# Second mixture's compaction on one Trainium2 core: slot indicators as weights, value columns moving

## The chip, the core and the metric

The kernel runs on one core of one Trainium2 chip. The metric is the device time of one execution in microseconds (us); three runs of the kernel before gave 768.0, 770.58 and 772.56, so the median is 770.58.

## What is computed

The reference has three parts. A linear attention with decay runs over 768 steps for 4 batches and 8 heads of width 48; its output, 3072 tokens of 384 numbers, goes through a first mixture of 8 experts (each token to its best expert, weighted by a gate), and the result through a second mixture, which gives every expert exactly 384 tokens:

```python
cap = N // E                       # 3072 / 8 = 384
order = np.argsort(-flat)          # all (token, expert) logits, best first
for idx in order:
    tok, e = (int(idx) // E, int(idx) % E)
    if assigned[tok] >= 0 or counts[e] >= cap:
        continue
    assigned[tok] = e
    counts[e] += 1
...
    h = np.maximum(x[mask] @ w1[e], 0.0)
    out[mask] = h @ w2[e]
```

## The kernel before, in words

The attention comes first, then the first mixture, then the second; the end of each overlaps with the start of the next. In the second mixture the greedy assignment is found expert by expert. For p = 0 to 7, `chain` (L1171) finds by counting the threshold at which the expert that fills up next is full. Each count is a few small matmuls into the PSUM tile `pcn` (L1230, L1238, L1243) with VectorE operations between them (`cmp`, `XC`, `FL`, `nn`, `wb`, `t`). The chain ends with `slot` (L1336), a number from 1 to 384 for every token of this expert and 0 for the others. Tokens lie on 128 partitions with J = 24 in each.

`compact` (L1370) then turns "a slot per token" into "a token per slot": the 384 row numbers that the gather wants, `ig`, the same for the scatter of the outputs, `ix`, and the gates of these tokens, `gg`. It does so with one-hot matmuls:

- `oq` (L1382, VectorE) is 128 x 128 x 24 in bf16: for partition and j, a 1 at the slot's place within its block of 128. The column index j is innermost, so the 128 entries of `oq[:, :, j]` lie 24 elements (48 bytes) apart.
- `VV` (L1379, GpSimd) holds for each token 18 values: for each of the three blocks of 128 slots the token's partition, its j, three bf16 parts of its gate, and a 1, all times the block's indicator `b3`.
- 24 matmuls (L1387) have `VV[:, j, :]`, 32 columns, as weights and `oq[:, :, j]`, 128 columns, moving. They go in turn to four groups of 32 columns of the array, so that `pq`, 128 x 128 in PSUM, holds four partial sums under one another.
- `cx` (L1389) is that as bf16 in SBUF. One more matmul (L1392), with `cx` as weights and the constant `FO` (128 x 6) moving, adds the four parts and forms row number and gate, and with it each slot comes to lie on its own partition. Three VectorE operations (L1394 to L1398) read `ig`, `ix` and `gg` from PSUM.

`FO` is made from `idq` by four VectorE operations (L1072 to L1075), which the scheduler puts near the start of the program. The three gathers (L1404, GpSimd) bring the tokens' rows to `xr`. `tin` (L1444) transposes them and splits them into `x2h` and `x2l`, and `compute` (L1455) runs the two layers of the expert as products of 384 columns: 24 groups of three, then three times 8 groups of three.

Order of the work: up to the call `in_order(True)` in `mixture` (L1513) the scheduler sets each engine's order by priorities; behind it every engine runs in program order. There `chain` and `compact` are generators, and each `yield n` says after how many groups of three products the next piece is put into the order (`step`, L1538). `compact` has a `yield 2` between `cx` and the last matmul. The chains of p = 0 and 1 and the first seven pieces of p = 2 stand ahead of `in_order(True)`, the rest beside the products of the experts. In the profile most instructions of the ordered part carry line L297, that of a helper, so they are told apart by their tiles. The weights of each expert come from HBM into `stage`, are split by ScalarE into `whi` and `wlo`, and a GpSimd DMA adds `stage` into `wlo` (L1438 to L1440).

Of the kernel before, what the change touches and what calls it, by code (L numbers as in the profile page):

```python
# [14 lines left out]
BF16 = mybir.dt.bfloat16  # L15
I32 = mybir.dt.int32
U32 = mybir.dt.uint32
AF = mybir.ActivationFunctionType
ALU = mybir.AluOpType
AX = mybir.AxisListType  # L20
# [7 lines left out]
N = B * S  # L28
E = 8
# [8 lines left out]
J = N // 128  # L38
# [47 lines left out]
def tile_kernel(ctx: ExitStack, tc, rd, kd, wd, r3, k3, w3, vd, ud, emb, tau, m1w1, m1w2, m1w2t, wg2, wgt, m2w1, m2w2, out):  # L86
    nc = tc.nc
    PSUM = bass.MemoryType.PSUM
    cst = ctx.enter_context(tc.tile_pool(name="cst", bufs=1))
# [9 lines left out]
    def bcast(ap, shape):  # L99
        return ap.to_broadcast(shape)  # L100
# [31 lines left out]
    id16 = cst.tile([128, 32], FP16, name="id16")  # L132
    idq = cst.tile([128, 32], F32, name="idq")
    VV = cst.tile([128, J, 32], BF16, name="VV")
    FO = cst.tile([128, 6], BF16, name="FO")
    prc = cst.tile([128, E], F32, name="prc")
    cnt1 = cst.tile([128, E], F32, name="cnt1")
    io24 = cst.tile([128, J], F32, name="io24")
# [21 lines left out]
    te, ve, se, gp = [nc.tensor], [nc.vector], [nc.scalar], [nc.gpsimd]  # L160
# [66 lines left out]
    with tc.tile_pool(name="ld", bufs=3) as ld, tc.tile_pool(name="wk", bufs=2) as wk, \  # L227
# [423 lines left out]
        a, b = NST - 2, NST - 1  # L651
# [39 lines left out]
        while ready:  # L691
# [9 lines left out]
                                op=ALU.is_gt)  # L701
# [117 lines left out]
    pcn = pcp.tile([128, 512], F32, name="pcn")  # L819
    with tc.tile_pool(name="m1", bufs=1) as mp, tc.tile_pool(name="ps1", bufs=2, space=PSUM) as ps:  # L820
# [247 lines left out]
        nc.vector.memset(fm, 0.0)  # L1068
        asg = ap_.tile([128, J], F32, name="asg")
        nc.vector.memset(asg, 0.0)  # L1070
        fo3 = idq[:, :18].rearrange("p (a b) -> p a b", a=3)
        nc.vector.scalar_tensor_tensor(FO[:, 0:3], fo3[:, :, 0], float(J), fo3[:, :, 1], op0=ALU.mult, op1=ALU.add)  # L1072
        nc.vector.scalar_tensor_tensor(FO[:, 0:3], fo3[:, :, 5], -4096.0, FO[:, 0:3], op0=ALU.mult, op1=ALU.add)
        nc.vector.tensor_add(FO[:, 3:6], fo3[:, :, 2], fo3[:, :, 3])
        nc.vector.tensor_add(FO[:, 3:6], FO[:, 3:6], fo3[:, :, 4])  # L1075

        ii = ap_.tile([2 * E, E], F32, name="ii")
        nc.vector.tensor_add(ii, ident[:2 * E, :E], ident[:2 * E, E:2 * E])
        pfree = ap_.tile([128, 128], F32, name="pfree")
# [57 lines left out]
    with tc.tile_pool(name="m2", bufs=2) as mp, tc.tile_pool(name="ps2", bufs=2, space=PSUM) as ps:  # L1137
# [4 lines left out]
        def small(shape, name, dt=F32, bufs=None):  # L1142
            bufs = bufs or 1 + (name in twin)
            return ck.tile(shape, dt, name=name, bufs=bufs)

        plan = {}
        first = [None]
        pcm = ps.tile([128, 512], F32, name="pcm", bufs=1)
# [22 lines left out]
        def chain(p, full):  # L1171
# [183 lines left out]
            with tc.high_priority(HK if p else HC + 1000) if first_ else ExitStack():  # L1355
                place()
                c = compact(p, slot)
                if first_:
                    for _ in c:
                        pass  # L1360
                else:
                    next(c)
# [7 lines left out]
        def compact(p, slot):  # L1370
            ge = small([128, 4, J], "ge")
            ve[0].tensor_tensor(ge, bcast(slot[:, None, :], [128, 4, J]), thr, op=ALU.is_ge)
            gs = small([128, J], "gs")
            ve[0].tensor_add(gs, ge[:, 1], ge[:, 2])
            pb16 = small([128, J], "pb16", BF16)
            ve[0].scalar_tensor_tensor(pb16, gs, -128.0, slot, op0=ALU.mult, op1=ALU.add)
            b3 = small([128, J, 3], "b3", BF16)
            gp[0].tensor_tensor(b3.rearrange("p j a -> p a j"), ge[:, 0:3], ge[:, 1:4], op=ALU.subtract)
            gp[0].tensor_tensor(VV[:, :, :18].rearrange("p j (a b) -> p j a b", a=3), bcast(b3[:, :, :, None], [128, J, 3, 6]),  # L1379
                                    bcast(val[:, :, None, :], [128, J, 3, 6]), op=ALU.mult)  # L1380
            oq = small([128, 128, J], "oq", BF16, bufs=1)
            ve[0].tensor_tensor(oq, ioq, bcast(pb16[:, None, :], [128, 128, J]), op=ALU.is_equal)  # L1382
            pq = pcm[:, :128] if p else pcn[:, 320:448]
            yield 0
            for j in range(J):
                q = j % 4
                te[0].matmul(pq[32 * q:32 * q + 32, :], VV[:, j, :], oq[:, :, j], start=(j < 4), stop=(j >= J - 4))  # L1387
            cx = small([128, 128], "cx", BF16)
            ve[0].tensor_copy(cx, pq)  # L1389
            pf = pcm[:, 260:266] if p else pcn[:, 456:462]  # L1390
            yield 2
            first[0] = te[0].matmul(pf, cx, FO, start=True, stop=True)  # L1392
            ig = small([128, 3], "ig", I32, bufs=2)
            ve[0].tensor_scalar(ig, pf[:, 0:3], 4096.0, N - 1.0, op0=ALU.add, op1=ALU.min)  # L1394
            ix = small([128, 3], "ix", I32, bufs=E)
            ve[0].tensor_scalar(ix, pf[:, 0:3], 4096.0, None, op0=ALU.add)
            gg = small([128, 3], "gg", bufs=E)
            ve[0].tensor_copy(gg, pf[:, 3:6])  # L1398
            d = plan[p]
            d["ix"] = ix  # L1400
            d["gg"] = gg
            xr = mp.tile([128, 3, DM], F32, name="x2")
            for a in range(3):
                d["got"] = gp[0].indirect_dma_start(out=xr[:, a, :], out_offset=None, in_=y1,  # L1404
                                                        in_offset=bass.IndirectOffsetOnAxis(ap=ig[:, a:a + 1], axis=0))
            d["xr"] = xr
# [227 lines left out]
```

## Time and profile before

| what | value |
|---|---|
| median of 3 runs | 770.58 us |
| the profiled execution, its own time | 765.87 us |
| its span | 763.8 us |
| mean granted TensorE clock | 0.964 of full speed |
| TensorE matmuls | 715.1 us busy, 94% of the span |
| VectorE | 474.3 us, 62% |
| ScalarE | 416.2 us, 54% |
| GpSimd | 316.4 us, 41% |

An engine's busy share is a mean over stages. The ends of matmuls are modelled, and matmuls overlap in the pipeline, so what one costs is read from the starts of the instructions around it. A row of a timeline gives start, length, engine, line, operation, tiles (out<-in), shapes and, in square brackets, idle time before it with what ended it. A row that merges n instructions ("x24") has the start of the first and the length to the end of the last. PE is TensorE, DVE VectorE, ACT ScalarE, POOL GpSimd, SP the DMA queue of the sync engine.

### The profile page before, as it was taken

To read this page: it belongs to the slowest core of one execution; us is meant where nothing else is said; L and a number is where in the kernel's file an instruction comes from. 1 tells how busy PE (TensorE), PEld (TensorE's weight loads), DVE (VectorE), ACT (ScalarE), POOL (GpSimd) and SP (SyncE) were. 2 spreads that over 40 slices of the span, in tenths; PEclk is the share of its full clock that TensorE was granted. 3 is DMA by queue.
4 is the path that set the end of the run, shared out by engine and by line. 5 is a ranking of instruction groups with operands and counts; after the bars stand their busy time and mean duration, and the time that the engine had idled before them with its cause. 6 is when DMAs were issued, how large, how long until landed. Compare 5 with 4: busy or idle time off the path is not lost.

```text
span 763.8 us, 15129 instructions
## 1 busy us (share of the span) xinstructions
PE 715.1 (94%) x5452; PEld 629.4 (82%) x5452; DVE 474.3 (62%) x1434; ACT 416.2 (54%) x887; POOL 316.4 (41%) x353
## 2 busy tenths in 40 slices
PE   5999999999799999999998999679989999999994
PEld 4888888887399999999986887358878888879994
DVE  8788979986332765666766757567455656461220
ACT  2687766565236585665754513226567565556730
POOL 6342665353102453454526304435364636365311
PEclk9999989999989999999998999869999999999998
DMA  8699996651555999999989604558999998999920
GB/s 263 209 257 253 293 277 186 199 161 53 166 184 113 245 257 250 251 235 277 228 203 217 150 1 137 123 176 195 260 230 287 261 247 246 199 251 271 236 62 35
DMA packets 54002, 155.50 MB, mean 204 GB/s; under 512 B 9297, under 2 KB 15939, under 8 KB 53916
## 3 DMA queue, kind: packets, MB, share of 16 engines
q0 software_dynamic: 25392, 69.32, 42.8%
q1 hardware_dynamic: 28044, 84.46, 34.4%
q8 instruction: 45, 0.74, 0.4%
q10 hardware_dynamic: 480, 0.64, 0.3%
q14 instruction: 41, 0.34, 0.1%
HBM read 84.56 MB, written 19.90 MB: 137 GB/s over the span
## 4 chain that ended last, share of the span: by engine, by line
PE 43%; issue 9%; DMA 8%; POOL 4%; DVE 4%; ACT 2%; SPq 0%; POOLq 0%; ACTq 0%; DVEq 0%
PE pH L297 32%; DMA wlo<-stage 3%; DMA stage<-in_m2w_dram 2%; PE pH L731 2%; PE pH L733 2%; PE pX L297 2%; PE pH L732 2%; PE pcm L297 1%; POOL out_dram L297 1%; DMA stage<-in_m1w_dram 1%; DMA xr<-xg 1%; PE pcn L297 1%; DMA lg<-lr,resti 1%; POOL wlo L178 1%; PE pO L297 1%
## 5 line engine op out<-in xcount | busy, mean ns | idle before, releaser
L297 ACT CAST whi<-stage 128x768 fp32r<-128x768 f32 x116 | 96.2, 830 | 10.6 <-DMA stage<-in_m2w_dram 10.5
L297 POOL DMA_DIRECT2D wlo<-stage x72 | 64.4, 913 | 83.7 <-ACT wlo L297 69.6
L297 ACT ACTIVATE wlo<-stage 128x768 fp32r<-128x768 f32 x116 | 98.2, 847 | 0.0
L178 POOL DMA_DIRECT2D wlo<-stage x52 | 46.8, 915 | 81.7 <-ACT wlo L297 76.1
L297 PE MATMUL pH<-x2h,whi 128*128 128x384 f32 x192 | 70.4, 367 | 0.0
L297 PE MATMUL pH<-whi,h2h 128*128 128x384 f32 x192 | 69.6, 363 | 0.0
L297 PE MATMUL pH<-x2l,whi 128*128 128x384 f32 x192 | 66.0, 344 | 0.4 <-DVE x2l L297 0.4
L297 PE MATMUL pH<-x2h,wlo 128*128 128x384 f32 x192 | 65.9, 343 | 0.5 <-DMA wlo<-stage 0.5
L297 PE MATMUL pH<-whi,h2l 128*128 128x384 f32 x192 | 65.6, 342 | 0.0
L297 PE MATMUL pH<-wlo,h2h 128*128 128x384 f32 x192 | 65.6, 341 | 0.0
L297 DVE SCALAR_TENSOR_TENSOR h2l<-pH,h2h 128x384 fp32r<-128x384 f32 x64 | 35.1, 555 | 39.0 <-ACT h2h L297 38.7
L297 POOL TENSOR_TENSOR z<-rd,kd 128x512 f32<-128x512 f32 x23 | 30.9, 1343 | 64.4 <-issue 17.5
L297 ACT ACTIVATE h2h<-pH 128x384 fp32r<-128x384 f32 x64 | 31.0, 487 | 47.2 <-PE pH L297 42.7
L297 PE MATMUL pH<-xhi,whi 128*128 128x416 f32 x144 | 53.6, 372 | 0.2 <-DVE hl L297 0.2
L297 PE MATMUL pH<-xlo,whi 128*128 128x416 f32 x144 | 51.6, 359 | 0.0
L297 PE MATMUL pH<-hh,whi 128*128 128x416 f32 x144 | 51.6, 359 | 0.0
L297 PE MATMUL pH<-xhi,wlo 128*128 128x416 f32 x144 | 51.5, 358 | 0.0
L297 PE MATMUL pH<-hl,whi 128*128 128x416 f32 x144 | 50.7, 352 | 0.5 <-DVE hl L297 0.5
L297 PE MATMUL pH<-hh,wlo 128*128 128x416 f32 x144 | 50.7, 352 | 0.0
L297 DVE SCALAR_TENSOR_TENSOR hl<-pH,hh 128x416 fp32r<-128x416 f32 x48 | 27.7, 587 | 34.8 <-ACT hh L297 34.5
L985 POOL DMA_INDIRECT y<-yr,ids x26 | 29.2, 1124 | 45.4 <-ACT yr L971 28.4
L297 ACT ACTIVATE cv<-vv,cs 128x48 f32<-128x48 f32 x192 | 45.9, 325 | 0.1
(457 smaller groups left out, 1908.8 us busy)
## 6 DMA issues: line engine op xcount, KB each, us to landing
wlo<-stage POOLq DMA_DIRECT2D x128, 384.0 KB, 6.4
stage<-in_m1w_dram SPq DMA_DIRECT2D x32, 768.0 KB, 5.5
stage<-in_m2w_dram SPq DMA_DIRECT2D x32, 768.0 KB, 6.6
xg<-zt SPq DMA_DIRECT2D x8, 627.2 KB
vv<-in_v_dram SPq DMA_DIRECT2D x24, 192.0 KB, 2.9
wz<-in_w_dram SPq DMA_DIRECT2D x42, 96.8 KB, 5.0
xr<-xg SPq DMA_DIRECT2D x21, 193.0 KB, 4.2
rd<-in_r_dram SPq DMA_DIRECT2D x42, 96.0 KB, 4.4
```

The lines of the kernel that those rows point to most:

```text
L178: nc.gpsimd.dma_start(lo[:, s].bitcast(F32), t[:, o:o + h // 2], accum_op=ALU.add)
L297: return tc.keep_in_program_order(f(*a, **k))
L731: te[0].matmul(o, wh, xh, start=start, stop=False)
L732: te[0].matmul(o, wh, xl, start=False, stop=False)
L733: pe[0] = te[0].matmul(o, wl, xh, start=False, stop=stop)
L985: s = nc.gpsimd.indirect_dma_start(out=dst, out_offset=bass.IndirectOffsetOnAxis(ap=ids, axis=0), in_=src, in_offset=None, bounds_check=N ...
```

## The change

Weights and moving operand change places. The 24 matmuls now load `oq[:, :, j]`, 128 columns at a step of 24 elements, as weights and move the 18 columns of `VV[:, j, :18]`; all 24 add into the same 128 x 18 of PSUM, where each slot already has its own partition. `cx`, `FO` and the second matmul are gone, and so is the `yield 2`. VectorE puts row number and gate together from PSUM: two operations for `at`, one for `ix`, one for `ig` (which now follows from `ix`), and a sum of three for `gg`.

```diff
-    FO = cst.tile([128, 6], BF16, name="FO")
...
-        fo3 = idq[:, :18].rearrange("p (a b) -> p a b", a=3)
-        nc.vector.scalar_tensor_tensor(FO[:, 0:3], fo3[:, :, 0], float(J), fo3[:, :, 1], op0=ALU.mult, op1=ALU.add)
-        nc.vector.scalar_tensor_tensor(FO[:, 0:3], fo3[:, :, 5], -4096.0, FO[:, 0:3], op0=ALU.mult, op1=ALU.add)
-        nc.vector.tensor_add(FO[:, 3:6], fo3[:, :, 2], fo3[:, :, 3])
-        nc.vector.tensor_add(FO[:, 3:6], FO[:, 3:6], fo3[:, :, 4])
...
-            pq = pcm[:, :128] if p else pcn[:, 320:448]
+            pq = pcm[:, :18] if p else pcn[:, 320:338]
             yield 0
             for j in range(J):
-                q = j % 4
-                te[0].matmul(pq[32 * q:32 * q + 32, :], VV[:, j, :], oq[:, :, j], start=(j < 4), stop=(j >= J - 4))
-            cx = small([128, 128], "cx", BF16)
-            ve[0].tensor_copy(cx, pq)
-            pf = pcm[:, 260:266] if p else pcn[:, 456:462]
-            yield 2
-            first[0] = te[0].matmul(pf, cx, FO, start=True, stop=True)
+                first[0] = te[0].matmul(pq, oq[:, :, j], VV[:, j, :18], start=(j == 0), stop=(j == J - 1))
+            c = pq.rearrange("p (a b) -> p b a", a=3)
+            at = small([128, 2, 3], "at")
+            ve[0].tensor_scalar(at[:, 0], c[:, 5], -4096.0, 4096.0, op0=ALU.mult, op1=ALU.add)
+            ve[0].scalar_tensor_tensor(at[:, 1], c[:, 0], float(J), at[:, 0], op0=ALU.mult, op1=ALU.add)
+            ix = small([128, 3], "ix", I32, bufs=E)
+            ve[0].tensor_tensor(ix, c[:, 1], at[:, 1], op=ALU.add)
             ig = small([128, 3], "ig", I32, bufs=2)
-            ve[0].tensor_scalar(ig, pf[:, 0:3], 4096.0, N - 1.0, op0=ALU.add, op1=ALU.min)
-            ix = small([128, 3], "ix", I32, bufs=E)
-            ve[0].tensor_scalar(ix, pf[:, 0:3], 4096.0, None, op0=ALU.add)
+            ve[0].tensor_scalar(ig, ix, N - 1.0, None, op0=ALU.min)
             gg = small([128, 3], "gg", bufs=E)
-            ve[0].tensor_copy(gg, pf[:, 3:6])
+            ve[0].tensor_reduce(gg, pq.rearrange("p (a b) -> p a b", a=3)[:, :, 2:5], axis=AX.X, op=ALU.add)
```

The change also moves instructions where the scheduler sets the order. The place that matters is the compaction of p = 1, beside which run the last transposes of expert 0's tokens and the first counts of the chain of p = 2 (its matmuls into `pcn`). On TensorE there stood before, ahead of the 24 compaction matmuls, the small matmul of `FL` that the count of p = 2 waits for:

```order
L297 MATMUL pH<-x2l,whi 128x384
L297 MATMUL pH<-x2h,wlo 128x384
L1243 LDWEIGHTS ones
L1243 MATMUL pcn<-FL_108,ones 128x8
L1387 LDWEIGHTS VV
L1387 MATMUL pcm<-oq,VV 32x128
```

Now the compaction stands directly behind the two products, and behind its last matmul come:

```order
L1379 MATMUL pcm<-VV,oq 128x18
L1236 LDWEIGHTS ones
L1236 MATMUL pcn<-FL_108,ones 128x8
L1223 LDWEIGHTS oh_6241
L1223 MATMUL pcn<-cmp,oh_6241 32x184
```

So the `FL` matmul has gone from ahead of the 24 matmuls to behind them. On VectorE, at the same place (`x2l` is the split of expert 0's tokens, `nn`, `wb`, `t` and `cmp` belong to the count of p = 2), the order before was:

```order
L724 TENSOR_TENSOR x2l<-pX,x2h 128x384
L1376 SCALAR_TENSOR_TENSOR pb_6181<-gs,slot 128x24
L1240 TENSOR_TENSOR FL_108<-pcn,need 46x8
L1382 TENSOR_TENSOR oq<-ioq,pb_6181 128x3072
L1245 TENSOR_REDUCE nn<-pcn 128x1
L724 TENSOR_TENSOR x2l<-pX,x2h 128x384
L1248 SCALAR_TENSOR_TENSOR wb<-nn,w_6250 128x24
L1251 TENSOR_SCALAR t_6271<-nn 128x1
L1217 TENSOR_TENSOR cmp<-wb,tblB 128x1104
L1389 CAST cx<-pcm 128x128
L1234 CAST XC_107<-pcn 128x4x46
```

And it is now, from `oq` on:

```order
L1375 TENSOR_TENSOR oq<-ioq,pb_6176 128x3072
L1233 TENSOR_TENSOR FL_108<-pcn,need 46x8
L723 TENSOR_TENSOR x2l<-pX,x2h 128x384
L1382 TENSOR_SCALAR at<-pcm 128x3
L1238 TENSOR_REDUCE nn<-pcn 128x1
L1383 SCALAR_TENSOR_TENSOR at<-pcm,at 128x3
L1241 SCALAR_TENSOR_TENSOR wb<-nn,w_6245 128x24
L1244 TENSOR_SCALAR t_6266<-nn 128x1
L1385 TENSOR_TENSOR ix<-pcm,at 128x3
L1389 TENSOR_REDUCE gg<-pcm 128x3
L1387 TENSOR_SCALAR ig<-ix 128x3
L1210 TENSOR_TENSOR cmp<-wb,tblB 128x1104
```

`FL` has gone behind `oq`, and `cmp`, which stood ahead of the first operation that reads the compaction's PSUM, has gone behind all five of them.

## Rows read from the trace of the kernel before

**Rows 1.** The page's first part: busy time, share of the span, instructions.
```profile
PE 715.1 (94%) x5452; PEld 629.4 (82%) x5452; DVE 474.3 (62%) x1434; ACT 416.2 (54%) x887; POOL 316.4 (41%) x353
```

**Rows 2.** Busy time by stretch: length, then busy us per engine, granted clock, DMA share, GB/s.
```profile
20.00:60.00 40.00, 39.67 (x536) 34.63 (x535) 32.68 (x59) 30.32 (x98) 16.13 (x20) 1.00 0.84 235
```
```profile
490.00:508.00 18.00, 8.63 (x70) 5.05 (x70) 12.80 (x56) 1.34 (x3) 7.01 (x8) 0.52 0.54 181
...
560.00:600.00 40.00, 40.00 (x267) 35.03 (x266) 25.00 (x90) 24.52 (x39) 21.52 (x23) 0.97 1.05 262
```

**Rows 3.** Timeline of TensorE around the compaction of p = 2.
```profile
525.78 1.51 PE L297 MATMUL pcm<-oq,VV 128*32 128x128 bf16 x24 [0.43 <-POOL VV L297]
527.22 0.45 PE L297 MATMUL pH<-whi,h2h 128*128 128x384 f32 x1
527.51 0.34 PE L297 MATMUL pH<-wlo,h2h 128*128 128x384 f32 x1
...
528.21 0.34 PE L297 MATMUL pH<-whi,h2l 128*128 128x384 f32 x1
528.38 0.18 PE L297 MATMUL pcm<-FO,cx 128*128 128x6 bf16 x1
...
528.68 0.34 PE L297 MATMUL pH<-wlo,h2h 128*128 128x384 f32 x1
```

**Rows 4.** Timeline of TensorE: four 16-bit weight loads of 128 columns; eight f32 ones.
```profile
454.83 0.35 PE L733 MATMUL pH<-hh,wlo 128*128 128x416 f32 x1
455.02 0.26 PE L1238 MATMUL pcn<-id,XC 128*128 128x8 f16 x4
...
455.41 0.35 PE L732 MATMUL pH<-hl,whi 128*128 128x416 f32 x1
```
```profile
22.07 1.05 PE L297 MATMUL kvb<-ub,z 128*128 128x2 f32 x8
```

**Rows 5.** Length of one matmul: by tile (ns min/median/max), then by group (busy, mean).
```profile
L297 PE MATMUL pcm<-oq,VV x144: 382/403/414, 525.8 to 684.8; 128*32 128x128 bf16 x144
```
```profile
L297 PE MATMUL pcn<-id,XC x72: 165/167/230, 509.4 to 661.5; 128*128 128x8 f16 x72
```
```profile
L297 PE MATMUL kvb<-ub,z 128*128 128x2 f32 x192 | 26.8, 262 | 2.6 <-POOL z L297 2.6
```

**Rows 6.** Timeline of TensorE around the compaction of p = 1.
```profile
502.07 1.52 PE L1387 MATMUL pcm<-oq,VV 128*32 128x128 bf16 x24 [1.27 <-DVE oq L1382]
503.47 0.49 PE L1230 MATMUL pcn<-cmp,oh 128*32 128x184 bf16 x6
...
506.85 0.49 PE L297 MATMUL pcn<-cmp,oh 128*32 128x184 bf16 x6 [1.76 <-DVE cmp L1217]
```

**Rows 7.** Timeline of TensorE: the same count matmuls later, at the full clock.
```profile
513.82 0.34 PE L297 MATMUL pcn<-cmp,oh 128*32 128x184 bf16 x6
514.09 0.44 PE L297 MATMUL pH<-x2h,whi 128*128 128x384 f32 x1
```

**Rows 8.** Timeline of VectorE around the compaction of p = 1.
```profile
499.14 0.55 DVE L724 TENSOR_TENSOR x2l<-pX,x2h 128x384 fp32r<-128x384 f32 x1
499.61 0.62 DVE L1376 SCALAR_TENSOR_TENSOR pb<-gs,slot 128x24 bf16<-128x24 f32 x1
...
500.26 1.76 DVE L1382 TENSOR_TENSOR oq<-ioq,pb 128x3072 bf16<-128x3072 bf16 x1
501.93 0.16 DVE L1245 TENSOR_REDUCE nn<-pcn 128x1 f32<-128x8 f32 x1
...
502.68 0.73 DVE L1217 TENSOR_TENSOR cmp<-wb,tblB 128x1104 bf16<-128x1104 f16 x1
503.64 0.29 DVE L1389 CAST cx<-pcm 128x128 bf16<-128x128 f32 x1 [0.23 <-PE pcm L1387]
504.00 0.35 DVE L1234 CAST XC<-pcn 128x184 f16<-128x184 f32 x1
504.26 0.15 DVE L1394 TENSOR_SCALAR ig<-pcm 128x3 int32<-128x3 f32 x1
504.33 0.15 DVE L1396 TENSOR_SCALAR ix<-pcm 128x3 int32<-128x3 f32 x1
```

**Rows 9.** Waits from 430 us on: total us, times, longest.
```profile
PE pH L297 <- DMA wlo<-stage: 0.5, 1, 0.5
```
```profile
DVE ig L297 <- PE pcm L297: 3.7, 5, 1.0
```

## The prediction

> **What bounds the kernel now.** I read the busy shares first: TensorE is busy 94% of the span, VectorE 62%, all others less [rows 1]. That is a mean, so the busy time by stretch comes next [rows 2]. From 560 to 600 us, in the middle of the second mixture, TensorE is busy for 40.00 of 40.00 us; DMA stands at 1.05 there, so a second resource is about as full. [...] The compactions of p = 2 to 7 lie in stretches of the first kind, where TensorE time is time of the kernel; that of p = 0 (474 us) lies among the last products of the first mixture, which TensorE also fills; only that of p = 1 (502 us) lies in the hollow, where a chain of waits between VectorE and TensorE sets the pace. So the question has two parts: what a compaction costs TensorE in seven places, and what the new order does to the chain at p = 1. For both I read timelines, and costs from the starts of neighbours, not from lengths.
>
> **What a compaction costs TensorE now.** At p = 2 the 24 matmuls start at 525.78 and the next product at 527.22, which is 1.44 us; the product behind it comes 0.29 later, where products otherwise start 0.175 apart (0.70 for the four steps from 527.51 to 528.21), so 0.115 more is lost [rows 3]: 1.555 us together. The second matmul, of `cx` and `FO`, sits between products that start at 528.21 and 528.68: 0.47 us for two steps of 0.175, so it costs 0.12. Sum: 1.675 us. The wait of 0.43 ahead of the compaction is for `VV` from GpSimd, which the change leaves as it is.
>
> **What it will cost.** Everything hangs on one price, which the trace has no row for: loading 128 bf16 weight columns that lie 48 bytes apart. I call x the time from one load-and-matmul pair to the next; a matmul of 18 columns is short beside it. I bound x from both sides, taking each time the length of a merged row less one matmul's own length, over the count less one.
>
> - Low end: the four pairs with `XC`, 128 columns of 16 bits side by side, take 0.26 us in all, one of them 0.167, so pairs come every (0.26 - 0.167) / 3 = 0.031 us [rows 4, 5].
> - One at a time: the eight f32 pairs with `z` come every (1.05 - 0.262) / 7 = 0.113 us [rows 4, 5]. So 16-bit weights load nearly four times as fast.
> - What the step costs: today's matmuls read this very `oq` as moving operand, and come every (1.51 - 0.403) / 23 = 0.048 us [rows 3, 5]. The count matmuls, which move 184 columns side by side into the same four column groups, need 0.27 us to the next product for all six [rows 7], about 0.045 each with the end included and with 56 more columns. The step makes itself felt, then. A second sign: at p = 1, in the hollow, the 24 matmuls take 1.40 us to the next start and so no longer than at the full clock, while the six count matmuls behind them take 0.49 in place of 0.34 [rows 6, 7]. So the reading of `oq` does not go by TensorE's clock.
> - High end: 0.048 us is with four groups reading at once; one reader at that rate needs 4 x 0.048 = 0.192 us.
>
> [...] The high end is kept for the range, and the low end too.
>
> [...]
>
> Behind the four `XC` pairs the loss is small: from 454.83 to 455.41 there are 0.58 us for two steps of 0.19 (454.83 to 455.02 is one), so 0.20 for four pairs, 0.08 more than 4 x 0.031 [rows 4]. A compaction will thus cost 24x + 0.08 = 1.23 us in place of 1.675: **-0.44 us** each, and for p = 0 and 2 to 7 together 7 x (24x - 1.595) = **-3.1 us**.
>
> **The compaction of p = 1.** Two things change there. `oq` comes earlier: it now follows the second `x2l` directly, which starts at 499.14 and hands over 0.47 later, and not `pb` and `FL`; so it runs from about 499.6 and not from 500.26 [rows 8], ends near 501.35, and the 24 matmuls run from 501.4 to 502.65 in place of 502.07 to 503.47. But the `FL` matmul is now queued behind them, and with it all that the count of p = 2 waits for. Before, `nn` came at 501.93, and `cmp` (502.68, 0.73 long) ran beside the compaction matmuls, so that the count's matmuls could follow at 503.47 and `XC` at 504.00 [rows 6, 8]. Now `nn` can start only near 502.95 (after the `FL` matmul); `wb`, which needs it, follows about 0.2 later, then `t` and the new `ix`, `gg` and `ig` at some 0.1 each (`ig` and `ix` start 0.07 apart [rows 8], and the new ones depend on one another), so `cmp` starts near 503.7 and ends near 504.4. The matmuls follow at 504.45 and `XC` at 504.98: **+1.0 us** against 504.00. Everything behind it in the hollow shifts along, up to the matmuls at 506.85, behind which the products of expert 0 are queued. If x is larger, this grows by 24 (x - 0.048).
>
> **The rest, at nothing.** The four `FO` operations near the start take VectorE up to 1 us; TensorE is busy for 39.67 of 40 us from 20 to 60 us [rows 2], so this gain stays hidden (at most 1 us faster if that cover were gone). `cx` (0.29 long) gives way to two more small operations; VectorE is not the bound. For p = 2 to 7 `at` waits for the compaction in the place where `cx` did; the second wait, `ig` for the `FO` matmul, 3.7 us in five times [rows 9], goes, so what is queued behind it (the next chain's first operations, the splits of hidden rows, and on GpSimd the gathers) comes a little sooner; nobody on the path waits for it. Some gathers move ahead of one weight DMA in GpSimd's queue. TensorE waited for `wlo` just once, for 0.5 us [rows 9], so this costs nothing unless a piece comes microseconds late.
>
> **Sum.** 7 x (24x - 1.595) + 1.0 + 24 (x - 0.048) = -3.1 + 1.0 = -2.1 us at x = 0.048. The sum is made against the profiled execution (765.87 us, span 763.8), which stands 4.7 us under the median of the runs. I put it on the median: 770.58 - 2.1 = **768.5 us**. No change can be told from one under about 0.5%, which is 3.85 us. The sum is zero at x = 0.059, -3.85 at x = 0.039, and +3.85 at x = 0.079.
>
> **The rivals.**
>
> 1. The step costs the weight load nothing, x = 0.031. For it: `XC` shows the fast load, and the profile counts loads in a lane of their own (PEld), apart from the moving columns. Against it: `oq` has been read slowly so far. Sum: 7 x (0.744 - 1.595) + 0.6 = -5.4 us, 765.2. Chance 0.20.
> 2. [...] Chance 0.28.
> 3. x is as forecast, but DMA takes the gain back: its share is 1.05 in the middle of the mixture [rows 2], so time that TensorE saves could turn into waits for `wlo`. Against it: that wait is 0.5 us in all. Then only p = 0 gains its 0.44 and p = 1 costs its 1.0: +0.6 us, 771.2. Chance 0.10.
>
> **How the numbers follow.** The forecast has 0.42; with rival 3 it makes up "within 0.5%", 0.52. Faster by more is rival 1, 0.20; slower by more is rival 2, 0.28. The range goes from rival 1 with some 1 us for the scatter of the runs, 764, to the one-at-a-time price, 781; what lies outside is the upper part of rival 2 and little else. The likeliest case alone, x from 0.039 to 0.079, has 766.7 to 774.4.
>
> **What would show it.** In the changed kernel's timeline the 24 pairs should hold TensorE for some 1.2 us to the next product, at p = 2 to 7 as at p = 1, with no small matmul two groups later. Near 500 us the `FL` matmul should stand behind the 24, and the second `XC` should come about 1 us later after the split of the tokens than now. If the 24 pairs take 0.8 us, it is rival 1; if they take 2.7 us or more, rival 2; if they take 1.2 and waits for `wlo` have grown by microseconds, rival 3. The forecast is wrong, whatever the time, if the difference comes from a stretch without a compaction.

## The result and the profile after

The changed kernel took 775.0 us (median of 19 executions), the kernel before 770.64 beside it (19): ratio 1.0054, 95% interval [1.0028, 1.0080], so **4.2 us slower (2.2 to 6.2)**. Ratios and intervals here leave out executions more than 1.5% above the fastest of their kernel. I had forecast 2.1 us less than before. Line numbers of the changed kernel are one or a few lower. The profiled execution has a span of 768.2 us, 4.4 over that of before. The busy shares answer [rows 1] and have hardly moved; PEld, the lane of weight loads, has grown by 9 us:

```profile
PE 715.0 (93%) x5444; PEld 638.7 (83%) x5444; DVE 474.6 (62%) x1438; ACT 416.3 (54%) x887; POOL 319.9 (42%) x353
```

The timeline of TensorE around the compaction of p = 2 answers [rows 3]:

```profile
527.74 1.77 PE L296 MATMUL pcm<-VV,oq 128*128 128x18 bf16 x24 [0.44 <-POOL VV L296]
529.37 0.42 PE L296 MATMUL pH<-whi,h2h 128*128 128x384 f32 x1
529.63 0.34 PE L296 MATMUL pH<-wlo,h2h 128*128 128x384 f32 x1
529.80 0.40 PE L296 MATMUL pH<-whi,h2l 128*128 128x384 f32 x1
530.00 0.53 PE L296 MATMUL pH<-whi,h2h 128*128 128x384 f32 x1
530.32 0.53 PE L296 MATMUL pH<-wlo,h2h 128*128 128x384 f32 x1
...
532.88 0.53 PE L296 MATMUL pH<-whi,h2h 128*128 128x384 f32 x1
533.20 0.42 PE L296 MATMUL pH<-wlo,h2h 128*128 128x384 f32 x1
```

Two things are to be seen. The 24 pairs hold TensorE for 1.63 us to the next product, where 1.44 was before. Their length by tile (the answer to [rows 5]) is 0.215 us:

```profile
L296 PE MATMUL pcm<-VV,oq x144: 170/215/219, 527.7 to 682.9; 128*128 128x18 bf16 x144
```

So a pair comes every (1.77 - 0.215) / 23 = **0.068 us**, not 0.048. And from 530.00 to 533.20 ten products come 0.32 apart in place of 0.175: 1.45 us lost. The windows of that stretch (columns as in [rows 2]) give the reason; the granted clock falls from 1.00 to 0.50 while TensorE is busy throughout:

```profile
527.00:529.00 2.00, 1.56 (x21) 1.41 (x20) 1.80 (x5) 0.61 (x1) 1.51 (x2) 1.00 0.79 151
529.00:531.00 2.00, 2.00 (x15) 1.99 (x15) 1.31 (x7) 0.00 (x0) 0.41 (x1) 0.74 1.13 194
531.00:533.00 2.00, 2.00 (x8) 2.00 (x7) 1.86 (x8) 0.00 (x0) 1.63 (x2) 0.50 0.89 316
533.00:535.00 2.00, 2.00 (x12) 2.00 (x11) 1.38 (x6) 1.88 (x3) 1.76 (x2) 0.91 0.80 293
```

The same happens behind the compactions of p = 6 (670.67) and p = 7 (681.33), and behind none of the kernel before. At p = 1, in the hollow (490 to 508 us in [rows 2]), the timelines of TensorE and VectorE answer [rows 6, 8]:

```profile
498.94 0.49 PE L1223 MATMUL pcn<-cmp,oh 128*32 128x184 bf16 x6
...
502.58 1.84 PE L1379 MATMUL pcm<-VV,oq 128*128 128x18 bf16 x24 [0.39 <-DVE oq L1375]
504.27 0.17 PE L1236 MATMUL pcn<-FL,ones 128*128 128x8 bf16 x1
505.94 0.49 PE L1223 MATMUL pcn<-cmp,oh 128*32 128x184 bf16 x6 [1.49 <-DVE cmp L1210]
...
509.33 0.49 PE L296 MATMUL pcn<-cmp,oh 128*32 128x184 bf16 x6 [1.78 <-DVE cmp L1210]
```
```profile
504.46 0.16 DVE L1382 TENSOR_SCALAR at<-pcm 128x3 f32<-128x3 f32 x1 [1.40 <-PE pcn L1236]
504.54 0.16 DVE L1238 TENSOR_REDUCE nn<-pcn 128x1 f32<-128x8 f32 x1
...
505.15 0.73 DVE L1210 TENSOR_TENSOR cmp<-wb,tblB 128x1104 bf16<-128x1104 f16 x1
506.47 0.35 DVE L1227 CAST XC<-pcn 128x184 f16<-128x184 f32 x1 [0.58 <-PE pcn L1223]
```

FL stands behind the 24, `nn` and `cmp` come after it. The first count matmuls of p = 2 start at 498.94, the third set at 509.33: 10.39 us. Before, the first set was

```profile
497.53 0.49 PE L1230 MATMUL pcn<-cmp,oh 128*32 128x184 bf16 x6
```

and the third came at 506.85 [rows 6], so 9.32. That is +1.07. The waits answer [rows 9]: no wait for `wlo` is left, and `ig` waits no more, but `at` does:

```profile
DVE at L296 <- PE pcm L296: 7.9, 6, 2.1
...
PE pcm L296 <- POOL VV L296: 1.0, 2, 0.5
```

So there are three candidates: the price of a pair, the order at p = 1, and the clock behind a compaction. A fourth I had not thought of came out of the runs: p = 0.

### The profile page after: what moved, and what is told of

It is laid out like the page before. It is cut to its first block, busy times and chain, and to the rows that moved or that the text cites. A ratio compares the mean times of both kernels' runs of the same rounds, so it can differ in the third digit from the quotient of the medians.

```text
span 768.2 us, 15113 instructions
## 1 busy us (share of the span) xinstructions
PE 715.0 (93%) x5444; PEld 638.7 (83%) x5444; DVE 474.6 (62%) x1438; ACT 416.3 (54%) x887; POOL 319.9 (42%) x353
## 4 chain that ended last, share of the span: by engine, by line
PE 44%; issue 9%; DMA 7%; POOL 5%; DVE 5%; ACT 2%; POOLq 0%; ACTq 0%; DVEq 0%; SPq 0%
PE pH L296 31%; DMA wlo<-stage 2%; PE pH L730 2%; PE pH L732 2%; DMA stage<-in_m1w_dram 2%; PE pH L731 2%; DMA stage<-in_m2w_dram 2%; PE pX L296 1%; PE pcm L296 1%; PE pcn L296 1%; POOL out_dram L296 1%; POOL wlo L177 1%; DMA lg<-lr,resti 1%; POOL b L296 1%; PE pO L296 1%
## 5 line engine op out<-in xcount | busy, mean ns | idle before, releaser
L296 ACT CAST whi<-stage 128x768 fp32r<-128x768 f32 x116 | 96.2, 829 | 10.4 <-DMA stage<-in_m2w_dram 10.4
```

Of the source, the lines that this page charges most:

```text
L296: return tc.keep_in_program_order(f(*a, **k))
```

## The experiments

One number returns below: **time at the lower clock**, 2 x (1 - mean granted clock) x span, since the traces of both kernels show two levels, 1.00 and 0.50 (so in the windows of the changed kernel from 529.60 and from 530.00, 0.20 us long). It is there for every execution, not only the profiled one. Over 279 executions of 22 groups (each kernel and each set of runs of the kernel before by itself) an execution that has 1 us more of it than its group takes 0.36 us more (standard error 0.03), or 0.30 without the 15 that lie furthest above their kernel's fastest. This is a fit and not a price: waits and the lower clock can come together (in the changed kernel TensorE is busy for 11.06 of 20.40 us from 492.40 us on, at 0.50), and the fit does not part them. "New" is the changed compaction, "old" that of the kernel before.

**Old at p = 0 and 1, new at p = 2 to 7** (run twice), **and the mirror** (the condition is then p > 1).

```diff
-            pq = pcm[:, :18] if p else pcn[:, 320:338]
+            if p < 2:
+                pq = pcm[:, :128] if p else pcn[:, 320:448]
...
+            else:
+                pq = pcm[:, :18] if p else pcn[:, 320:338]
...
```

> The compactions of p = 0 and 1 as in the kernel before (with FO), those of p = 2 to 7 as in the changed kernel. Theory 'clock' (the changed compaction takes TensorE the same 1.7 us as the old one, but behind it the granted clock falls to its lower level for some 3.2 us where TensorE had waited just before it; three times, 1.5 us each): the loss stays, 2.5 to 5 us above the kernel before, and in the trace at least two of the six compactions are followed by some ten products 0.32 us apart. Rival 'hollow' (the loss comes from p = 1, where the FL matmul is queued behind the 24 pairs): within 1 us of the kernel before. Rival 'pairs' (six times 24 pairs at a price above the old one): the pairs at p = 2 to 7 take 2.3 us or more to the next product; the trace of the changed kernel has 1.63, so 0.2 us in all.

> The kernel with old p = 0 and 1 and changed p = 2 to 7 once more, on this chip, beside the delayed one. It was 0.9953 [0.9919, 0.9986] of the kernel before. Theory 'wait, then loads' wants it 0 to 3 us above the delayed one, by the falls behind p = 2, 6 and 7. If it stands above the kernel before here, the first figure was scatter.

> The mirror: p = 0 and 1 as in the changed kernel, p = 2 to 7 as in the kernel before. Theory 'clock': only p = 1 costs, 1 to 1.7 us above the kernel before, and no compaction is followed by products 0.32 apart. Rival 'hollow': 3 to 5 us above.

Measured: old at p = 0 and 1 gave 0.9953 [0.9919, 0.9986] and, on another chip, 1.0008 [0.9972, 1.0045]; the mirror 1.0038 [1.0005, 1.0072], that is +2.9 us. Theory "clock" as I had put it falls: with the six changed compactions alone the loss is gone, although both profiled executions show falls of the clock behind p = 2, 6 and 7. The loss goes with p = 0 and 1. "Pairs" falls as well: they take 1.61 to 1.63 us to the next product.

**The changed kernel again, twice.** The first of these was meant as a delay, but its edit had no effect: the number of the first yield in `compact` is dropped by the `next(c)` in `chain`, so instructions and order are those of the changed kernel.

```diff
-            yield 0
+            yield 3
             for j in range(J):
```

> The changed kernel with three groups of products more between the making of VV and oq and the 24 pairs of p = 2 to 7, so that TensorE does not wait for VV (0.44 and 0.53 us at p = 2 and 7) ahead of them. Theory 'clock': with the waits gone at least two of the three falls of the clock go, 3 us or more under the changed kernel, 0 to 1.5 above the kernel before. Rival 'loads alone lower the clock': the falls stay, the time is that of the changed kernel within 1.5 us. Rival 'hollow': the same, within 1.5 us of the changed kernel, whatever the clock does.

> The changed kernel itself once more, beside the next kernels on one chip, for the granted clock of each execution. Theory 'hollow plus clock' (1.07 us from the order at p = 1, some 0.14 us less for each of seven compactions, the rest of the loss from more time at the lower clock): 2 to 6 us above the kernel before, and over its executions at least 3 us more at the lower clock than the kernel before. Rival 'no clock': 0 to 1 us above, and the same time at the lower clock within 2 us.

Measured: 1.0068 [1.0031, 1.0104] and 1.0096 [1.0062, 1.0131], and 9.3 and 10.8 us more at the lower clock than the kernel before beside them (standard errors 2.3 and 2.6). The loss is real, and by that slope some 3 to 3.6 us of it go with the clock. Both profiles have no fall behind p = 2 to 7, but one behind **p = 0**, a place that I had costed as TensorE time alone. Timeline and windows of the first of the two:

```profile
477.16 1.77 PE L1379 MATMUL pcn<-VV,oq 128*128 128x18 bf16 x24 [1.46 <-POOL VV L1372]
478.79 0.67 PE L732 MATMUL pH<-whi,hl 128*128 128x384 f32 x1
479.25 0.53 PE L730 MATMUL pH<-whi,hh 128*128 128x384 f32 x1
479.57 0.53 PE L731 MATMUL pH<-wlo,hh 128*128 128x384 f32 x1
...
481.94 0.42 PE L1223 MATMUL pcn<-cmp,oh 128*32 128x184 bf16 x6
...
495.80 0.16 PE L1298 MATMUL pcn<-rs,tri 128*128 128x1 bf16 x1 [1.35 <-DVE rs L1295]
```
```profile
477.00:479.00 2.00, 1.84 (x25) 1.84 (x25) 0.35 (x2) 0.40 (x1) 1.02 (x2) 0.94 0.61 198
479.00:481.00 2.00, 2.00 (x7) 2.00 (x8) 1.14 (x10) 1.47 (x3) 0.71 (x1) 0.50 0.83 152
```

The first count matmuls of p = 1 (`cmp`, 481.94) are queued behind the slow products. From the 24 pairs to the `rs` matmul of p = 1 it takes 18.64 us; in the kernel before, 491.48 - 474.14 = 17.34, at a granted clock of 1.00:

```profile
474.14 1.53 PE L1387 MATMUL pcn<-oq,VV 128*32 128x128 bf16 x24 [0.95 <-POOL VV L1379]
...
491.48 0.17 PE L1305 MATMUL pcn<-rs,tri 128*128 128x1 bf16 x1 [1.35 <-DVE rs L1302]
```
```profile
474.00:476.00 2.00, 1.86 (x26) 1.02 (x27) 0.58 (x2) 1.06 (x2) 1.06 (x2) 1.00 0.09 36
476.00:478.00 2.00, 2.00 (x18) 1.44 (x16) 0.79 (x9) 1.88 (x4) 1.12 (x2) 1.00 1.01 187
```

In all profiles where the columns of `oq` lie 48 bytes apart at p = 0 this stretch takes 17.1 to 17.4 us without a fall behind p = 0, and 18.6 to 19.7 with one. So a fall there costs 1.3 us or more. The profile of the changed kernel from the section before is one without: 17.15 us.

**The step of `oq`.** Entries of one j side by side (in the constant `ioq` too), first as weights, then in the kernel before as moving operand.

```diff
-            oq = small([128, 128, J], "oq", BF16, bufs=1)
-            ve[0].tensor_tensor(oq, ioq, bcast(pb16[:, None, :], [128, 128, J]), op=ALU.is_equal)
+            oq = small([128, J, 128], "oq", BF16, bufs=1)
+            ve[0].tensor_tensor(oq, ioq, bcast(pb16[:, :, None], [128, J, 128]), op=ALU.is_equal)
```

> The changed kernel with oq and ioq laid out so that the 128 entries of one j lie side by side (2 bytes apart in place of 48). Theory 'step' (the step of 48 bytes sets the price of a pair, 0.068 us): pairs come every 0.03 us as those of XC do, the 24 take 0.75 to 0.95 us to the next product in place of 1.63, so 0.7 to 0.9 us less at each of seven places; oq on VectorE may take longer than its 1.75 us, up to about twice, since pb is then repeated along the innermost index, which costs up to 1.7 us at p = 1. Sum 3 to 6 us under the changed kernel. Rival 'full-width load' (a load of 128 rows by 128 columns in a run of 24 takes 0.068 us however the columns lie): pairs still 0.065 to 0.07 apart, and the time the same or, by oq, longer.

> The kernel before with oq and ioq laid out so that the 128 entries of one j lie side by side; there they are the moving operand. Theory 'step' (the moving side's 0.048 us is set by the step of 48 bytes, as I read it in the prediction): its 24 matmuls come 0.035 us apart or less. Rival 'rate' (0.048 is what 128 moving columns into one of four column groups take): 0.045 us or more. oq takes 3.36 us on VectorE, so the time is 5 us or more above the kernel before.

Measured at p = 2, first as weights, TensorE's timeline and the group of `oq` on VectorE (busy, mean ns of one, idle time before):

```profile
535.88 0.74 PE L296 MATMUL pcm<-VV,oq 128*128 128x18 bf16 x24 [2.04 <-POOL VV L296]
536.48 0.42 PE L296 MATMUL pH<-whi,h2h 128*128 128x384 f32 x1
```
```profile
L296 DVE TENSOR_TENSOR oq<-ioq,pb 128x3072 bf16<-128x3072 bf16 x6 | 20.1, 3358 | 0.2
```

Then as moving operand, the timeline and the group of these matmuls:

```profile
527.76 0.52 PE L297 MATMUL pcm<-oq,VV 128*32 128x128 bf16 x24 [2.02 <-POOL VV L297]
528.21 0.45 PE L297 MATMUL pH<-whi,h2h 128*128 128x384 f32 x1
```
```profile
L297 PE MATMUL pcm<-oq,VV 128*32 128x128 bf16 x144 | 3.1, 221 | 10.6 <-POOL VV L297 7.7 <-DVE fr L297 2.8
```

A pair takes (0.74 - 0.171) / 23 = 0.025 us and a moving matmul (0.52 - 0.221) / 23 = 0.013. So the step sets both prices: 0.068 against 0.025, and 0.048 against 0.013. The times are no gain, 1.0124 [1.0074, 1.0173] for the weights, because VectorE now takes 3.36 us for `oq` in place of 1.76 and TensorE waits: 13.0 us at p = 2 to 7 in the first kernel. The other was run once, 776.15 us beside a median of 774.52, which says nothing of the 5 us expected. The clock falls here too: in the first kernel behind six of the seven compactions outside the hollow, which last only 0.60 us but come after waits of 1.6 to 3.1 us; in the second, after waits of 1.0 to 2.0, behind one of seven. So a fall does not need the step of 48 bytes.

**Side by side with 24 small comparisons** (old at p = 0 and 1).

```diff
+                for j in range(J):
+                    ve[0].tensor_scalar(oq[:, j, :], io1, pb16[:, j:j + 1], None, op0=ALU.is_equal)
```

> p = 0 and 1 as in the kernel before; at p = 2 to 7 oq lies with the 128 entries of one j side by side, and VectorE makes it by 24 comparisons of 128 entries with one number of a partition each, in place of one comparison of 3072. Theory 'step': pairs come every 0.026 us as in the run with side-by-side columns, the 24 take 0.6 us to the next product in place of 1.63, six times 1.0 us: 5 to 7 us under the kernel with old p = 0 and 1 (about 8 us under the kernel before) if the 24 comparisons take no longer than the 1.76 us of the one (24 x 0.07, the spacing of small VectorE operations, is 1.7). Rival 'VectorE is late' (each of the 24 takes 0.1 us or more, so 2.4 us or more): TensorE waits for oq ahead of the pairs, as it did in the side-by-side run (waits for VV and fr of 13 us in six places), and most of the gain is lost: within 3 us of the kernel before.

Measured: 1.0092 [1.0056, 1.0129], so 7.1 us above the kernel before. The mechanism is that of "VectorE is late", the size is not: it had the time within 3 us of the kernel before. The 24 comparisons at p = 2 take 4.89 us, 0.20 each and not 0.07, and the pairs follow them, so that TensorE is held 2.60 us to the next product (timelines of VectorE and of TensorE):

```profile
526.57 4.89 DVE L297 TENSOR_SCALAR oq<-io,pbf 128x128 bf16<-128x128 bf16 x24
```
```profile
528.96 2.75 PE L297 MATMUL pcm<-VV,oq 128*128 128x18 bf16 x24
531.56 0.65 PE L297 MATMUL pH<-whi,h2h 128*128 128x384 f32 x1
```

**The pairs twice at p = 2 to 7.**

```diff
+            if p > 1:
+                for j in range(J):
+                    te[0].matmul(pcm[:, 200:218], oq[:, :, j], VV[:, j, :18], start=(j == 0), stop=(j == J - 1))
```

> The changed kernel with the 24 pairs of p = 2 to 7 done twice (the second set into unused columns of the same PSUM tile). Theory 'pairs': each further set of 24 takes 24 x 0.068 = 1.63 us of TensorE and all of it shows: 9.8 us above the changed kernel. Theory 'clock' adds to it: with 3.3 us of loads in a row the clock falls behind nearly every compaction, 1.5 us each, so 13 to 19 us above the changed kernel. Rival 'hidden': under 5 us above.

Measured: 790.84 us (1.0193 [1.0142, 1.0243]), 10.4 above the changed kernel on the same chip, so by time "pairs". In the profile the clock falls behind each of the six compactions, as "clock" said. The two don't add up to one figure here (four executions). At p = 2, where the slow products start at 542.23:

```profile
538.54 3.40 PE L296 MATMUL pcm<-VV,oq 128*128 128x18 bf16 x48 [0.45 <-POOL VV L296]
541.79 0.42 PE L296 MATMUL pH<-whi,h2h 128*128 128x384 f32 x1
...
542.23 0.52 PE L296 MATMUL pH<-whi,h2l 128*128 128x384 f32 x1
```

**Spread or delayed pairs.** Spread: old at p = 0 and 1, products between the pairs at p = 2 to 7. Delayed: three groups later, in the changed kernel, in the kernel before, and with old p = 0 and 1.

```diff
                 first[0] = te[0].matmul(pq, oq[:, :, j], VV[:, j, :18], start=(j == 0), stop=(j == J - 1))
+                if j % 6 == 5 and j < J - 1:
+                    yield 1
```
```diff
             yield 0
+            yield 3
```

> p = 0 and 1 compacted as in the kernel before; p = 2 to 7 as in the changed kernel, but with one group of three products after each 6 of the 24 pairs. Theory 'clock' (24 weight loads in a row, with little moving behind them, let the granted clock fall): no fall behind a compaction at p = 2 to 7, 1 to 3 us under the kernel before. Rival 'any interruption' (it is the waits of 0.4 to 0.8 us just ahead, not the run of loads): the falls stay, and the time is that of the kernel with old p = 0 and 1 within 1.5 us. Each of the three extra returns to the products costs about 0.085 us, so 0.255 us a compaction and 1.5 us in all for either.

> The changed kernel with three groups of products more ahead of the 24 pairs at p = 2 to 7 (about 1.6 us), this time really in the order. Theory 'wait, then loads' (the clock falls behind a compaction when TensorE has just waited and then does 1.7 us of weight loads; in the profiles so far 0 falls behind the compactions of p = 4 and 5, which it reaches without a wait, and about half at p = 2, 6 and 7 with waits of 0.4 to 0.8 us): the waits ahead of the pairs are under 0.2 us, no clock falls behind the compactions of p = 2 to 7, and the time is 2.5 to 4.5 us under the changed kernel (waits of 2.4 us less, falls of 1.45 us less), so 1 to 4 us above the kernel before, for p = 0 and 1 remain. Rival 'loads alone': falls still behind two or more.

> The same three groups in the kernel before, as a control: what the waits ahead of the compaction alone are worth. They were 1.1 us in all (0.43, 0.26 and 0.40 us), so 0 to 1.5 us under the kernel before. If it gains 3 us or more, the delay does something else than take away waits.

> p = 0 and 1 as in the kernel before, p = 2 to 7 changed and three groups later. Theory 'wait, then loads': no falls behind p = 2 to 7, nothing lost at p = 0 and 1, waits of 1.1 us and six times 0.14 us gained: 1 to 5 us under the kernel before, under both kernels. Rival: no better than the kernel before within 1 us.

Measured: 1.0098 [1.0056, 1.0140] spread; delayed 1.0118 [1.0083, 1.0152] (changed), 1.0061 [1.0023, 1.0099] (before, the control) and 1.0063 [1.0028, 1.0097] (old p = 0 and 1). In time all these theories fall by the control: the delay alone costs the kernel before 4.7 us. TensorE has new waits: 5.1 us for `cmp` in one wait in the spread kernel, 5.3 and 5.0 in the delayed ones with new pairs; the control waits 5.1 us for `h2l` and 2.7 for `wlo`. With the same delay, new against old at p = 0 and 1 is 1.0118 against 1.0063, and new against old at p = 2 to 7 is 1.0063 against 1.0061: again it is p = 0 and 1.

For the clock the delay did more. The waits directly ahead of the pairs are gone, and the clock falls behind one of the twelve delayed compactions of p = 2 to 7 (behind one of six in the spread kernel). That one, at p = 2 of the delayed changed kernel, does not speak against "wait, then loads", since two products ahead of the pairs TensorE had waited for `wlo` there (in the other delayed kernel it waited 0.54 us at the same place, and no fall followed):

```profile
529.14 0.44 PE L296 MATMUL pH<-wlo,h2h 128*128 128x384 f32 x1 [0.58 <-DMA wlo<-stage]
...
529.60 1.84 PE L296 MATMUL pcm<-VV,oq 128*128 128x18 bf16 x24
531.29 0.67 PE L296 MATMUL pH<-whi,h2h 128*128 128x384 f32 x1
```
```profile
531.00:533.00 2.00, 2.00 (x12) 2.00 (x12) 1.35 (x8) 0.36 (x1) 0.49 (x1) 0.51 0.88 201
```

**FO put back, FL put ahead, both.** The first keeps the four unused FO operations, the second gives the compaction of p = 1 the lowest priority.

```diff
-HK = 2000
+HK = 0
```

> The changed kernel with the four FO operations of VectorE put back near the start; nothing uses their result. In four of the five profiles without them the granted clock rose near 11 us and fell again near 14 us for 3.4 to 6.8 us, and by 25 us VectorE ran 0.7 us (once 1.3) behind the kernel before; in the five profiles with them that fall is missing. Theory 'start': the fall is gone, VectorE stands within 0.3 us of the kernel before at 25 us, and the time is some 0.7 us under the changed kernel, 2 to 6 us above the kernel before. Rival 'chance' (the fall near 14 us has nothing to do with FO): the fall is there again.

> The changed kernel with the compaction of p = 1 at the lowest priority, which puts the FL matmul and the first operations of the count of p = 2 ahead of the 24 pairs again. Theory 'hollow': from the first count matmuls of p = 2 to the third set 9.3 us in place of 10.39, 1.07 us under the changed kernel. Rival 'compaction late': the gathers of p = 1 come later for it, and the products of expert 1 wait: no gain.

> Both: FO put back and the compaction of p = 1 at the lowest priority. What is left of the change is then the pairs at p = 0 and 2 to 7, some 0.14 us less each, and what they do to the clock. Theory 'start and hollow': 1.8 us under the changed kernel, and within 2 us of the kernel before. Rival 'clock at p = 2 to 7': 3 us or more above the kernel before, with falls of the clock behind two or more of these compactions.

Measured: 1.0074 [1.0035, 1.0113], 1.0080 [1.0041, 1.0118], 1.0081 [1.0046, 1.0115]. Nothing is won. The early fall of the clock is missing in the first kernel and there again in the third, both with FO: chance. With FL ahead the first to third count matmuls still take 10.36 us, since `oq` then runs later (from 510.97, 1.75 us long) and the count matmuls stand behind the pairs. So the queue place of FL is not what the 1.07 us hang on; the count matmuls come behind the pairs in either order.

**Old at p = 1 alone, old at p = 0 alone.** The first diff with `p == 1` or `p == 0`.

> Only p = 1 compacted as in the kernel before; p = 0 and p = 2 to 7 as in the changed kernel. The order at p = 1 (the FL matmul behind the 24, oq ahead of FL) is there again, though p = 1 itself is unchanged: it comes from p = 0, whose shorter VectorE part the scheduler places otherwise. Theory 'p = 0 carries the loss' (by the order that it sets at p = 1, about 1 us, and by a fall of the clock behind its pairs, which lie in the chain, 1.3 to 2.4 us where it comes): from the first to the third count matmuls of p = 2 10.0 us or more in place of 9.32, a fall of the clock behind the compaction near 475 us, and 2 to 5 us above the kernel with old p = 0 and 1 (0.9953 and 1.0008 of the kernel before), so 0.2 to 0.6% above the kernel before. Rival 'p = 1 carries it' (its pairs at 0.068 us at the lower clock): within 0.2% of the kernel before.

> Only p = 0 compacted as in the kernel before; p = 1 to 7 as in the changed kernel. FL then stands ahead of the 24 pairs of p = 1, as before. Theory 'p = 0 carries the loss': from the first to the third count matmuls of p = 2 9.3 to 9.7 us (24 pairs hold TensorE 1.69 us there in place of 1.40, so 0.3 us more at most), no fall near 475 us, and the time within 0.3% of the kernel before, on either side. Rival 'p = 1 carries it': 10.3 us there and 0.4% or more above the kernel before.

Measured on one chip: new at p = 0, old at p = 1: **1.0103** [1.0056, 1.0151]; old at p = 0, new at p = 1: **1.0031** [0.9999, 1.0062]. The time at the lower clock is 17.0 and 5.6 us above the kernel before (standard errors 3.0 and 1.9). So most of the loss comes with p = 0, though the intervals overlap. The theory comes out in part: the first kernel lies above the 0.2 to 0.6% that it gave, and in its profiled execution there is no fall behind p = 0. And at p = 1 both pay, where the theory had 9.3 to 9.7 us for the second: 10.53 us from first to third count matmuls with old p = 1, whose order is now that of the changed kernel, and 10.71 with new p = 1 and FL ahead, where `at`, the first reader of the pairs' result, stands ahead of `cmp` and waits. TensorE of the first, then VectorE of the second:

```profile
510.43 1.52 PE L1388 MATMUL pcm<-oq,VV 128*32 128x128 bf16 x24 [0.39 <-DVE oq L1382]
511.89 0.19 PE L1243 MATMUL pcn<-FL,ones 128*128 128x8 bf16 x1
...
513.83 0.49 PE L1230 MATMUL pcn<-cmp,oh 128*32 128x184 bf16 x6 [1.29 <-DVE cmp L1217]
```
```profile
509.99 0.16 DVE L1407 TENSOR_SCALAR at<-pcm 128x3 f32<-128x3 f32 x1 [1.28 <-PE pcm L1404]
...
510.13 0.72 DVE L1217 TENSOR_TENSOR cmp<-wb,tblB 128x1104 bf16<-128x1104 f16 x1
```

**All together.** Falls of the clock within 4.5 us from the start of a compaction, counted in the profiled executions, with the 48-byte step throughout; at p = 2 to 7 without the spread, doubled and delayed kernels unless said:

| compaction | new | old |
|---|---|---|
| p = 0 (in every kernel with that step) | 6 of 10 | 1 of 8 |
| p = 2, 6, 7 | 6, 7, 5 of 10 | none of 9 (delayed one included) |
| p = 3, 4, 5 | none of 30 | none of 9 |
| p = 2 to 7, pairs twice | 6 of 6 | |
| p = 2 to 7, delayed (two kernels) | 1 of 12 | |
| p = 2 to 7, spread | 1 of 6 | |

| kernel | ratio | us at the lower clock above before |
|---|---|---|
| new everywhere (four runs, one with FO) | 1.0054, 1.0068, 1.0096, 1.0074 | (no clock on record beside it), 9.3, 10.8, 13.6 |
| new everywhere, FL ahead (two runs, one with FO) | 1.0080, 1.0081 | 12.8, 13.1 |
| old at p = 1 | 1.0103 | 17.0 |
| old at p = 0 | 1.0031 | 5.6 |
| old at p = 2 to 7 | 1.0038 | 3.2 |
| old at p = 0 and 1 (two runs) | 0.9953, 1.0008 | -1.5, 2.4 |

No version beat both kernels: old at p = 0 and 1 was ahead in one run and level in the other.

The profiles show three things more.

- **Waits and falls.** With the 48-byte step every fall behind single pairs at p = 2 to 7 had a wait of 0.44 us or more just ahead. At p = 4 and 5, reached with at most 0.27 us of waiting, it fell in none of 20 cases. At p = 3, reached after 0.57 to 0.70 us, it fell in none of 10 either, so such a wait is not enough. At p = 0 the six falls of the new compaction came after waits of 1.46 to 1.65 us for `VV`; the four cases without had 1.00, 1.00, 1.10 and 1.57. With the pairs twice it fell at p = 5 after a wait of 0.15.
- **Where the time lies.** From the start of the compaction of p = 0 to that of p = 2, four profiles with old p = 0 and 1 take 51.5 to 52.6 us, nine with new p = 0 take 52.4 to 56.1, in the mean 2.7 more; the one with new p = 1 alone takes 54.7 (side-by-side and delayed kernels left out). Behind p = 2, without the spread and doubled pairs too, the profiles scatter: 238.0 and 241.3 us to the end with the old compaction there, 238.8 to 244.7 with the new, and no price can be read.
- **Where the lower clock lies.** The stretch of lower clock in the hollow lasts 20.5 us in all seven profiles with old p = 0 and 1 and the 48-byte step there, and 23.9 in ten of the eleven with a new one (not in the first profile of the changed kernel). With the falls of the table, 3.4 us each, this makes some 3 + 2 + 6 = 11 us more at the lower clock, beside the 9.3 to 13.6 measured for the changed kernel.

## Why the prediction was wrong

- **x = 0.048 in the sum: the term was mis-sized.** No run shows this value for a pair: it was 0.068 us with the columns 48 bytes apart and 0.025 with them side by side. The bounds held, and the step matters as I read it. But 0.048 is the spacing of the moving matmuls, which go to four column groups, and it was no measure for these loads: the same step took the moving side from 0.013 to 0.048. By 7 x (24x - 1.595) the gain of 3.1 us turns into a loss of 7 x 0.037 = 0.3 us. The profiles show neither. From the start of a compaction to the fifteenth product behind it, less waits, other small matmuls and 14 steps of 0.1755 us, the six places p = 2 to 7 together cost 10.6 us before and 10.4 in the mirror, and 10.6 and 10.5 in the two repeats of the changed kernel, which have no fall there. (The recorded expectations go by 0.14 us less for each; that came from a sum over the whole stretch in one pair of profiles, and these six places do not bear it out.)
- **"The compaction of p = 1": +1.0 forecast, +1.07 measured**, in the row and at the place named. In part this is luck: by its own term 24 (x - 0.048) the forecast should have been 1.5 at the measured x. That FL stands behind the 24 was not the reason by itself, and the order comes from p = 0: it is there with p = 1 unchanged (10.53 us). With p = 0 unchanged the new p = 1 pays as much for another reason (10.71 us, `at` ahead of `cmp`).
- **"That of p = 0 (474 us) lies among the last products of the first mixture, which TensorE also fills": this step failed.** I costed p = 0 as TensorE time and gave it a gain of 0.44. The chain of p = 1 runs through those products, and what slows them slows the chain: 1.3 us or more where the clock fell behind the pairs. The runs that differ at p = 0 show the loss going with it: old there 0.9953, 1.0008 and 1.0031, new there 1.0038 to 1.0103 (single pairs with the 48-byte step, neither spread nor delayed).
- **A term was missing.** The sum holds every product at 0.175 us. Behind the 24 pairs the granted clock fell in 24 of 40 cases at four places (p = 0, 2, 6, 7), each time for 3.4 us (once for twice as long); at p = 2, 6 and 7 a fall cost 1.1 to 1.6 us within the next 14 products, 1.45 in the rows shown. The view to see it was there, since [rows 2] have the clock of the hollow; I asked of the loads how long they take, not what the clock does behind them.
- Rivals: DMA took nothing back, and there is no wait for `wlo`. Rival 2, slower by more, is the one that came nearest: the sum is zero at x = 0.059, and at the measured 0.068 it gives +1.7 us (0.3 from seven places, 1.0 + 0.5 from p = 1, where the trace has 1.07 in all). It has the sign, and 2.5 us of the 4.2 are missing in it.

What adds up: pairs 0 at p = 2 to 7, +1.07 at p = 1, falls behind p = 0 (0.6 x 1.3 = 0.8) and behind p = 2, 6 and 7 (18 in 10 profiles, 1.8 x 1.45 = 2.6): +4.5 us, against 4.2 [2.2, 6.2]. The total fits, the places do not. By this sum the kernels with old p = 0 and 1 should stand 2.6 us above the kernel before, and they stood at -3.6 [-6.3, -1.1] and +0.6 [-2.2, +3.5]; the mirror should stand at 1.9, and stood at 2.9 [0.4, 5.6]; the kernel with old p = 1 alone should stand at 4.5, and stood at 7.9 [4.3, 11.6].

So that most of the loss goes with p = 0 and 1 is shown, and that part of it is the order at p = 1 and falls behind p = 0 is read from rows; how much each is worth is argued. **What stays open:** whether the falls behind p = 2, 6 and 7 cost the program anything. Both profiles with old p = 0 and 1 have three of them, which is 10 us at the lower clock, and yet their executions have -1.5 and +2.4 us more than the kernel before; a profile is one execution, and how often the clock falls in the others is known only as a sum over the whole span. Open too is what decides whether it falls: a wait just ahead goes with it but is not enough, and the delay that took the waits away, and nearly all the falls, brought waits of its own.

## What to carry to other kernels

Here the weights paid for a step in memory (0.068 us a pair against 0.025), and so did the moving operand (0.048 against 0.013). Before a swap, price the operand by its own layout, with a row of that layout in that role, or measure it alone before anything else. The cost of these 24 loads with 18 columns moving was not over when the last one ended: at p = 0, 2, 6 and 7 the granted clock fell behind 24 of 40 (at p = 3, 4 and 5 behind none of 30). So look at the clock behind such a stretch, and ask of every place what chain is queued behind the products that then run slow. In a program ordered by a scheduler, an edit at one place can set the order at another (with new p = 0 and old p = 1, FL stood behind the 24 of p = 1, 10.53 us in place of 9.32), so change the places one by one.

## What I had not expected of the hardware

- A step of 48 bytes made a pair of weight load and 18-column matmul 2.7 times as long (0.068 against 0.025 us), and a 128-column moving operand 3.7 times (0.048 against 0.013).
- TensorE was busy for 2.00 of 2.00 us while its granted clock was at 0.50 (the windows at p = 2 above): the clock fell 2.2 us after TensorE's last wait, of 0.44 us, behind 1.6 us of loads. Behind 3.25 us of them it fell in six cases of six.
- VectorE took 3.36 us to make `oq` with the repeated operand along the innermost index, and 1.76 with it along the middle one, for the same 3072 results; a comparison of 128 entries with one number per partition took 0.20 us.
